# Spectral layer one sequence at a time, with output steps of sequence 0 between the mix items of sequence 1

## The chip, the cores and the metric

One core of one Trainium2 chip runs the whole program. The metric is device time in microseconds (us) of one execution. The kernel before was timed in three runs: 1540.98 us is the median, 1530.98 the lowest, 1542.16 the highest. A measurement of this kernel can tell about 1% (15.4 us) from no change.

## The reference: what is computed

Three layers run one after another; the change touches the first.

```python
# 1: spectral layer, x is (4 sequences, 3072 positions, 256)
X = np.fft.rfft(x, axis=1)
Yr = Xr @ w_r - Xi @ w_i + b_r
Yi = Xr @ w_i + Xi @ w_r + b_i
Yr, Yi = softshrink(Yr, 0.01), softshrink(Yi, 0.01)
y = np.fft.irfft(Yr + 1j * Yi, n=3072, axis=1)
# 2: top-1 mixture of 8 experts with a fixed capacity per expert (384 places)
# 3: dense mixture of 8 experts, weighted by a Sinkhorn-normalised gate
```

The places of layer 2 are given out in order of position, so with these inputs only the first two sequences (0 and 1) can hold a place; the kernel computes sequences 2 and 3 only in a branch that is taken if an expert is not full.

## The kernel before, in words

**The spectral layer** splits a 3072-point transform into 96 times 32. For each sequence there are four stages:

- `dft_in(b, i)`, 16 pieces: four matmuls on the input (tiles `xc`, four chunks of 8 rows per partition) with a 96-point matrix, split into a high and a low part (`z_hi`, `z_lo`) by ScalarE and VectorE.
- 24 *items* (b, u). `mix` multiplies by the weights: six matmuls of 512 columns (line 158). `fwd`: six matmuls of 256 columns with the matrix tile `mf` (line 179), then bias and soft shrink in `y` and `c` (lines 183 to 185; the last subtraction on VectorE for items that `solo` names, else on GpSimd). `shrink_split` splits `y` into `yh` and `yl`. `inv`: three matmuls of 256 columns with the matrix tile `mi` (line 200); ScalarE copies the result to `d` (line 202, two buffers), and SyncE's queue writes it to a DRAM tile `ds[b]` (line 203).
- A round trip through DRAM: `load_chunk` (line 118) reads `ds[b]` back in another order, as four chunks of 768 KB, into the same four `xc` tiles. A chunk holds rows of all 24 items, so the first chunk can be read only after the last item is written.
- `DftOut.step(k)`, 16 *output steps* per sequence, numbered through both sequences (k = 0 to 31, and two more that drain the pipeline). A step splits a piece of a chunk for step k + 2 (`dh`, `dl`), multiplies by `fi` (three matmuls of 512 columns, line 234), copies to `xo` (line 237) and writes `xs_d`, transposes the `xo` of step k - 1 (line 245), and multiplies the transposed piece of step k - 2 by the gate weights (`lps`, line 254). `out_step` adds the choice of experts for every fourth step (`choose`, `weigh`).

**The order** is written out by hand; each engine runs its instructions in program order. `mix_items` runs a software pipeline: iteration i issues `shrink_split` of item i - 4, `fwd` of i - 2, `mix` of i, `inv` of i - 5, three *fill* slots between them, and then a list `todo[i]`, which holds the loads of matrices, the loads of chunks and the output steps. `load_mats` runs on GpSimd's queue; with n buffers the load for a group waits until the group n places earlier has been used.

In the kernel before, the items run in five stretches: items 0 to 5 of sequence 0, the same of sequence 1, then items 6 to 13 of both in pairs that share one load of `mf` and `mi`, then 14 to 23 of sequence 0, and of sequence 1. So there are 40 groups of matrices for 48 items. Sequence 0 ends 10 items before sequence 1. Its first two chunks are read at iterations 42 and 43; output steps 0 to 5 stand at iterations 47 to 52, beside the last items, and steps 6 to 33 follow alone. Behind `mix_items` GpSimd clears `xg`, 128 x 6144 (line 534). The placing of tokens, the gather and the two expert layers follow; they are not touched.

## Time and profile before

| what | value |
|---|---|
| runs | 1530.98, 1540.98, 1542.16 us |
| profiled execution, span from first to last instruction | 1540.5 us |
| TensorE busy (matmul) | 1506.7 us, 98% |
| VectorE, ScalarE, GpSimd busy | 741.2, 484.9, 269.8 us |
| granted TensorE clock, mean | 0.958 of full speed |
| moved by DMA | 94.63 MB |

The profiled execution's time is given as its span alone; it lies 0.5 us below the median run, and nothing else is known to lie around it. Stretches are named by microseconds from the start of the span. The first transforms run to 22, the items and the transforms of sequence 1 from 28 to 163, the output steps to 273, the placing to 300, and the expert layers from 300 to the end. [...]

### The profile page before, as it was taken

To read this page: it belongs to the slowest core of one execution; us is meant where nothing else is said; L and a number is where in the kernel's file an instruction comes from. 1 tells how busy PE (TensorE), PEld (TensorE's weight loads), DVE (VectorE), ACT (ScalarE), POOL (GpSimd) and SP (SyncE) were. 2 spreads that over 40 slices of the span, in tenths; PEclk is the share of its full clock that TensorE was granted. 3 is DMA by queue.
4 is the path that set the end of the run, shared out by engine and by line. 5 is a ranking of instruction groups with operands and counts; after the bars stand their busy time and mean duration, and the time that the engine had idled before them with its cause. 6 is when DMAs were issued, how large, how long until landed. Compare 5 with 4: busy or idle time off the path is not lost.

```text
span 1540.5 us, 23165 instructions
## 1 busy us (share of the span) xinstructions
PE 1506.7 (98%) x9578; PEld 1376.4 (89%) x9578; DVE 741.2 (48%) x1451; ACT 484.9 (31%) x939; POOL 269.8 (18%) x330
## 2 busy tenths in 40 slices
PE   8999799799999999999999999999999999999998
PEld 7988688699999999999999999999999999999998
DVE  4768635665548444444444444444444444444443
ACT  3444554355542242222222222221222222132221
POOL 2354124642221010010101001010100101010122
PEclk8999855699999999999999999999999999999999
DMA  9447652353330220202000000000000000000000
GB/s 240 110 126 181 167 144 89 97 167 117 117 128 1 110 81 29 110 1 96 1 28 28 1 28 1 28 1 28 28 1 28 1 28 1 28 1 4 25 28 28
DMA packets 57159, 94.63 MB, mean 61 GB/s; under 512 B 5846, under 2 KB 39286, under 8 KB 55606
## 3 DMA queue, kind: packets, MB, share of 16 engines
q1 hardware_dynamic: 41622, 71.09, 14.7%
q0 software_dynamic: 14656, 21.71, 5.3%
q8 instruction: 76, 1.25, 0.3%
q10 hardware_dynamic: 768, 0.28, 0.1%
q14 instruction: 37, 0.30, 0.1%
HBM read 64.75 MB, written 28.31 MB: 60 GB/s over the span
## 4 chain that ended last, share of the span: by engine, by line
PE 78%; DMA 2%; issue 1%; POOLq 0%; DVE 0%; ACT 0%; ACTq 0%
PE ps_h L670 38%; PE ps_y L800 34%; PE ps_yT L694 4%; DMA out_dram<-acc,ido 1%; PE lg L679 1%; PE ps_t L658 0%; DMA xg<-xs_d,idx 0%; POOLq L959 0%; PE ps_s L771 0%; DVE hl L673 0%; ACT hh L672 0%; DVE xg L649 0%; ACT xgh L87 0%; POOLq L810 0%; PE ps_b L753 0%
## 5 line engine op out<-in xcount | busy, mean ns | idle before, releaser
L800 PE MATMUL ps_y<-w,hh 128*128 128x256 f32 x3072 | 557.3, 283 | 0.0
L672 ACT ACTIVATE hh<-ps_h 128x512 fp32r<-128x512 f32 (+2 forms) x456 | 262.8, 576 | 874.0 <-PE ps_h L670 873.6
L670 PE MATMUL ps_h<-x_hi,w 128*128 128x512 f32 (+1 forms) x1568 | 494.4, 387 | 0.0
L800 PEld LDWEIGHTS ps_y<-w,hh 128*128 128x128 f32 x3072 | 483.1, 189 | 7.7
L673 DVE SCALAR_TENSOR_TENSOR hl<-ps_h,hh 128x512 fp32r<-128x512 f32 (+2 forms) x456 | 301.8, 662 | 382.1 <-ACT hh L672 382.0
L800 PE MATMUL ps_y<-w,hl 128*128 128x256 f32 x1536 | 437.6, 285 | 0.0
L670 PEld LDWEIGHTS ps_h<-x_hi,w 128*128 128x128 f32 x1568 | 292.8, 188 | 58.4
L808 DVE SCALAR_TENSOR_TENSOR acc<-ps_y,pr,acc 128x256 f32<-128x256 f32 x360 | 174.2, 484 | 270.8 <-PE ps_y L800 259.6
L670 PE MATMUL ps_h<-x_lo,w 128*128 128x512 f32 (+1 forms) x784 | 303.5, 387 | 0.0
L800 PEld LDWEIGHTS ps_y<-w,hl 128*128 128x128 f32 x1536 | 290.3, 189 | 0.0
L88 POOL TENSOR_TENSOR w<-raw,w 128x512 fp32r<-128x512 f32 x84 | 109.4, 1304 | 953.9 <-ACT w L87 886.1
L670 PEld LDWEIGHTS ps_h<-x_lo,w 128*128 128x128 f32 x784 | 147.3, 188 | 25.5
L670 PE MATMUL ps_h<-xgh,w 128*128 128x384 f32 x256 | 78.0, 347 | 0.2 <-ACT xgh L87 0.2
L694 PE MATMUL ps_yT<-hh,w 128*128 128x384 f32 x256 | 75.8, 338 | 0.0
L87 ACT CAST w<-raw 128x512 fp32r<-128x512 f32 x124 | 75.5, 613 | 0.0
L670 PEld LDWEIGHTS ps_h<-xgh,w 128*128 128x128 f32 x256 | 48.0, 191 | 0.6 <-ACT xgh L87 0.6
L694 PEld LDWEIGHTS ps_yT<-hh,w 128*128 128x128 f32 x256 | 47.3, 188 | 0.0
L87 ACT CAST mh<-ps_m 128x512 fp32r<-128x512 f32 x48 | 28.2, 587 | 58.5 <-PE ps_m L158 58.5
L88 DVE TENSOR_TENSOR ml<-ps_m,mh 128x512 fp32r<-128x512 f32 x48 | 33.1, 690 | 27.6 <-ACT mh L87 27.6
L810 POOL DMA_INDIRECT out_dram<-acc,ido x24 | 23.4, 975 | 123.2 <-DVE acc L808 95.5
L670 PE MATMUL ps_h<-xgl,w 128*128 128x384 f32 x128 | 43.8, 342 | 0.0
L694 PE MATMUL ps_yT<-hl,w 128*128 128x384 f32 x128 | 43.2, 338 | 0.0
(169 smaller groups left out, 1313.4 us busy)
## 6 DMA issues: line engine op xcount, KB each, us to landing
raw<-in_moe_w_dram SPq DMA_DIRECT2D x60, 512.0 KB, 4.4
out_dram<-zt SPq DMA_DIRECT2D x24, 512.0 KB, 8.3
mf<-in_c_mats_dram POOLq DMA_DIRECT2D x40, 192.0 KB, 3.2
ds<-d SPq DMA_DIRECT2D x48, 128.0 KB, 2.7
xc<-ds SPq DMA_DIRECT2D x8, 768.0 KB, 5.9
xs_d<-xo SPq DMA_DIRECT2D x32, 192.0 KB, 2.1
xc<-in_x_dram SPq DMA_DIRECT2D x7, 768.0 KB, 12.7
mi<-in_c_mats_dram POOLq DMA_DIRECT2D x40, 128.0 KB, 2.9
```

The source lines that it names most:

```text
L87: nc.scalar.copy(hi_ap, src)
L88: (lo_engine or nc.vector).tensor_sub(lo_ap, src, hi_ap.bitcast(F32))
L670: nc.tensor.matmul(ps[:, 0:n], l, r[:, h, cols], start=k == 0, stop=k == 5)
L672: nc.scalar.activation(hh, ps[:, 0:n], AF.Relu)
L673: nc.vector.scalar_tensor_tensor(hl, ps[:, 0:n], 0.0, hh.bitcast(F32), op0=ALU.max, op1=ALU.subtract)
L679: nc.tensor.matmul(lg2[:, t, 0:m], src[:, h, c], wg2r[:, h, 0:m], start=i == 0, stop=i == 3)
L694: nc.tensor.matmul(yT[e][c], l, r, start=fk == 0 and i == 0, stop=fk == 2 * NF - 1 and i == 2)
L800: nc.tensor.matmul(ps, l, r, start=i == 0, stop=i == 3 * NF - 1)
L808: nc.vector.scalar_tensor_tensor(a, ps, pr[:, ti, e:e + 1], a, op0=ALU.mult, op1=ALU.add)
L810: nc.gpsimd.indirect_dma_start(out=out, out_offset=bass.IndirectOffsetOnAxis(ap=ido[:, ti % NCH, ti // NCH:ti // NCH + 1], axis=0), in_=a, ...
```

## The change

The items run one sequence at a time: 24 of sequence 0, then 24 of sequence 1, each with its own load of `mf` and `mi` (48 groups; `mf` has four buffers instead of five). The 16 `dft_in` pieces of sequence 1 are spread over 23 iterations instead of filling the first six. All four chunks of sequence 0 are read at iterations 29 and 30. Output steps 0 to 11 stand at iterations 32 to 51, between items of sequence 1. Two chunks of sequence 1 are read at iteration 52, the others in steps 12 and 15. Steps 12 to 33 follow `mix_items`. The last subtraction of the shrink goes to VectorE for four items only (26 before). `mh`, `ml` get three buffers and `dh`, `dl` two of their own (four shared before); `xo` has three instead of four.

```diff
-    mfp = s1.enter_context(tc.tile_pool(name="mfp", bufs=5))
+    mfp = s1.enter_context(tc.tile_pool(name="mfp", bufs=4))
...
-        mh = wk.tile([128, 2 * D], F32R, tag="mh", name="mh", bufs=4)
-        ml = wk.tile([128, 2 * D], F32R, tag="ml", name="ml", bufs=4)
+        mh = wk.tile([128, 2 * D], F32R, tag="mh", name="mh")
+        ml = wk.tile([128, 2 * D], F32R, tag="ml", name="ml")
...
-            dh = wk.tile([128, 2 * D], F32R, tag="mh", name="dh", bufs=4)
-            dl = wk.tile([128, 2 * D], F32R, tag="ml", name="dl", bufs=4)
+            dh = wk.tile([128, 2 * D], F32R, tag="dh", name="dh", bufs=2)
+            dl = wk.tile([128, 2 * D], F32R, tag="dl", name="dl", bufs=2)
...
-                o = w2p.tile([P1, 2, D], F32, tag="xo", name="xo", bufs=4)
+                o = w2p.tile([P1, 2, D], F32, tag="xo", name="xo", bufs=3)
...
-            todo.setdefault(max(last[g - 5] + 2, 0) if g >= 5 else 0, []).append(lambda g=g: load_mats(groups, g, True))
+            todo.setdefault(max(last[g - 4] + 2, 0) if g >= 4 else 0, []).append(lambda g=g: load_mats(groups, g, True))
...
-    UA, UB = 6, 14
-    items, groups = [], []
-    for b, u0, u1 in ((0, 0, UA), (1, 0, UA), (None, UA, UB), (0, UB, NU), (1, UB, NU)):
-        for u in range(u0, u1):
-            its = [(b, u)] if b is not None else [(0, u), (1, u)]
-            items += its
-            groups.append((u, its))
+    items = [(b, u) for b in range(NP) for u in range(NU)]
+    groups = [(u, [(b, u)]) for b, u in items]
...
-    i_d0 = items.index((0, NU - 1)) + 5
+    i_d0 = NU + 5
     todo = {}
     od = DftOut((0, 1))
-    todo.setdefault(i_d0, []).extend([lambda: load_chunk(ds[0], 0)])
-    todo.setdefault(i_d0 + 1, []).append(lambda: load_chunk(ds[0], 1))
-    early = [-1, 0, 1, 2, 3, 4]
-    for k, i in enumerate(early):
-        todo.setdefault(n_it + i, []).append(lambda k=k: out_step(k))
+    for g in range(4):
+        todo.setdefault(i_d0 + g // 2, []).append(lambda g=g: load_chunk(ds[0], g))
+    EARLY = 12
+    first = i_d0 + 3
+    for k in range(EARLY):
+        todo.setdefault(first + (k * (n_it + 5 - first)) // EARLY, []).append(lambda k=k: out_step(k))
+    for g in range(2):
+        todo.setdefault(n_it + 4, []).append(lambda g=g: load_chunk(ds[1], g))
...
-        if k in (1, 4):
-            load_chunk(ds[0], 2 + k // 4)
-        if k in (8, 9, 13, 17):
-            load_chunk(ds[1], (8, 9, 13, 17).index(k))
+        if k in (12, 15):
+            load_chunk(ds[1], 2 + (k - 12) // 3)
...
-    mix_items(items, groups, 2, 1, todo, solo=lambda i: UA <= i < 2 * UA or i >= n_it - 2 * (NU - UB),
-              fill=[lambda i=i: dft_in(1, i) for i in range(16)])
+    spread = []
+    for i in range(16):
+        spread += [lambda i=i: dft_in(1, i)] + [lambda: None] * (4 if i % 2 else 3)
+    mix_items(items, groups, 2, 1, todo, solo=lambda i: i >= n_it - 4, fill=spread)
```

**TensorE, output steps.** Before, from step 6 on, the steps of TensorE's queue stand one behind another (`ps_x` is the product of a step, `ps_t` its transposes, `lps` the gate logits):

```order
L234 MATMUL ps_x<-dh,fi 96x512
L234 MATMUL ps_x<-dl,fi 96x512
L234 MATMUL ps_x<-dh,fi 96x512
L245 MATMUL ps_t<-ident,xo 128x96 x4
L254 MATMUL lps<-wg1s,xT 96x8 x4
L234 MATMUL ps_x<-dh,fi 96x512
L234 MATMUL ps_x<-dl,fi 96x512
L234 MATMUL ps_x<-dh,fi 96x512
L245 MATMUL ps_t<-ident,xo 128x96 x4
L254 MATMUL lps<-wg1s,xT 96x8 x4
```

Now, at iterations 32 to 47, a step stands between the `inv` of one item and the `fwd` of another:

```order
L200 MATMUL ps_d<-yh,mi 128x256
L234 MATMUL ps_x<-dh,fi 96x512
L234 MATMUL ps_x<-dl,fi 96x512
L234 MATMUL ps_x<-dh,fi 96x512
L245 MATMUL ps_t<-ident,xo 128x96 x4
L254 MATMUL lps<-wg1s,xT 96x8 x4
L179 MATMUL ps_y<-mh,mf 128x256
L179 MATMUL ps_y<-ml,mf 128x256
L179 MATMUL ps_y<-mh,mf 128x256 x2
L179 MATMUL ps_y<-ml,mf 128x256
L179 MATMUL ps_y<-mh,mf 128x256
L158 MATMUL ps_m<-w_hi,z_hi 128x512
```

Nine steps (0 to 8) now stand ahead of the last `mix`, and three more (9 to 11) among the last `fwd` and `inv`; before, step 0 was the first behind the last `mix`.

**SyncE's queue, the read of sequence 0** (`ds_171` is `ds[0]`, `ds_172` is `ds[1]`, `xc0` to `xc3` are the chunks). Before, one write of an item stands between two chunks, and the other chunks come 8 and 15 rows later, between output steps:

```order
L203 DMA ds_171<-d_1937 128x256
L118 DMA xc0_111<-ds_171 96x2048
L203 DMA ds_172<-d_1976 128x256
L118 DMA xc1_112<-ds_171 96x2048
L203 DMA ds_172<-d_2015 128x256
L203 DMA ds_172<-d_2053 128x256
```

Now four chunks stand within seven rows:

```order
L203 DMA ds_172<-d_1473 128x256
L118 DMA xc0_111<-ds_171 96x2048
L118 DMA xc1_112<-ds_171 96x2048
L203 DMA ds_172<-d_1513 128x256
L118 DMA xc2_113<-ds_171 96x2048
L118 DMA xc3_114<-ds_171 96x2048
L203 DMA ds_172<-d_1553 128x256
L203 DMA ds_172<-d_1591 128x256
```

The first write behind a chunk now has two chunks ahead of it, and the next has four.

**GpSimd, the clearing of `xg`.** Before, it stands directly behind the last load of a matrix:

```order
L126 DMA mf<-in_c_mats_dram 128x384
L129 DMA mi<-in_c_mats_dram 128x256 x4
L534 MEMSET xg 128x6144
L291 CAST g_2396<-gw 96x8
L292 TENSOR_TENSOR r<-gw,g_2396 96x8
```

Now it stands behind the `weigh` of output step 11 (iteration 51), which needs `gw` from VectorE:

```order
L291 CAST g_2535<-gw 96x8
L292 TENSOR_TENSOR r<-gw,g_2535 96x8
L293 TENSOR_SCALAR g_2535<-r 96x8
L294 TENSOR_SCALAR r_2537<-g_2535 96x8
L295 TENSOR_TENSOR r_2537<-r_2537,r 96x8
L296 TENSOR_SCALAR g_2535<-r_2537 96x8
L299 TENSOR_TENSOR val<-oh,hc 96x64x2
L302 TENSOR_TENSOR val<-oh,g_2535 96x64x3
L532 MEMSET xg 128x6144
```

The clearing has moved from iteration 47 to behind the last output step of `mix_items`.

## Rows read from the trace of the kernel before

**Rows 1.** Busy time by stage (x instructions), PEclk granted clock, DMA share, GB/s.

```profile
27.95:158.00 130.05, 129.99 (x803) 116.52 (x803) 91.81 (x214) 58.45 (x144) 51.89 (x90) 0.97 0.61 150
158.00:163.20 5.20, 3.78 (x19) 2.59 (x18) 2.45 (x7) 2.24 (x6) 0.57 (x1) 1.00 0.94 228
163.20:171.10 7.90, 0.49 (x2) 0.18 (x2) 7.83 (x7) 1.50 (x4) 5.75 (x2) 0.78 0.17 51
174.50:184.60 10.10, 8.91 (x73) 7.74 (x72) 5.54 (x12) 7.48 (x19) 0.00 (x0) 1.00 0.67 197
184.60:272.90 88.30, 88.30 (x425) 75.20 (x425) 37.18 (x115) 44.07 (x90) 29.24 (x63) 0.50 0.42 122
```

**Rows 2.** TensorE in order of time: start, length, instruction; the last items.

```profile
153.42 0.28 PE L179 MATMUL ps_y<-mh,mf 128*128 128x256 f32 x1
...
154.13 0.40 PE L158 MATMUL ps_m<-w_hi,z_hi 128*128 128x512 f32 x1
...
155.53 0.28 PE L200 MATMUL ps_d<-yh,mi 128*128 128x256 f32 x1
...
155.89 0.28 PE L179 MATMUL ps_y<-mh,mf 128*128 128x256 f32 x1
...
157.77 0.40 PE L158 MATMUL ps_m<-w_hi,z_lo 128*128 128x512 f32 x1
```

**Rows 3.** TensorE in order of time, output steps beside the last items.

```profile
176.32 0.40 PE L234 MATMUL ps_x<-dh,fi 128*96 128x512 f32 x1
...
177.99 0.37 PE L200 MATMUL ps_d<-yh,mi 128*128 128x256 f32 x1
...
183.50 0.38 PE L200 MATMUL ps_d<-yh,mi 128*128 128x256 f32 x1 [1.19 <-ACT d L202]
```

**Rows 4.** TensorE in order of time, the last output steps.

```profile
264.70 0.84 PE L245 MATMUL ps_t<-ident,xo 96*128 96x96 f32 x4
...
266.53 0.72 PE L234 MATMUL ps_x<-dh,fi 128*96 128x512 f32 x1
...
269.73 0.88 PE L245 MATMUL ps_t<-ident,xo 96*128 96x96 f32 x4
```

**Rows 5.** SyncE's queue in order of time, around the first two chunk reads.

```profile
152.13 0.32 SPq L118 DMA_DIRECT2D xc<-ds  x1
152.51 0.42 SPq L203 DMA_DIRECT2D ds<-d  x1
152.97 0.43 SPq L118 DMA_DIRECT2D xc<-ds  x1
154.15 10.57 SPq L203 DMA_DIRECT2D ds<-d  x4
```

**Rows 6.** ScalarE in order of time: the copies to d behind those reads.

```profile
158.65 0.37 ACT L202 COPY d<-ps_d 128x256 f32<-128x256 f32 x1 [2.33 <-DMA ds<-d]
...
162.12 0.37 ACT L202 COPY d<-ps_d 128x256 f32<-128x256 f32 x1 [2.31 <-DMA ds<-d]
```

**Rows 7.** VectorE in order of time, at the clearing of xg.

```profile
163.63 5.74 DVE L184 TENSOR_SCALAR c<-y 128x256 f32<-128x256 f32 x1
```

**Rows 8.** GpSimd in order of time, the clearing of xg.

```profile
163.98 5.24 POOL L534 MEMSET xg<- 128x6144 f32 x1
```

**Rows 9.** The page's DMA issues: KB each, us to landing, writes of items.

```profile
ds<-d SPq DMA_DIRECT2D x48, 128.0 KB, 2.7
```

**Rows 10.** Tile xc, issue at 195.48: time to landing of one chunk read.

```profile
DMA to landing us min/median/max: 5.9/5.9/5.9
```

**Rows 11.** Groups by line, 184.60 to 272.90: count, busy us, mean ns, idle before.

```profile
L237 ACT COPY xo<-ps_x 96x512 f32<-96x512 f32 x27 | 15.7, 582 | 31.2 <-PE ps_x L234 31.2
L87 ACT CAST dh<-xc 128x512 fp32r<-128x512 f32 x25 | 15.5, 619 | 0.0
```

**Rows 12.** Groups by line, 60 to 158, GpSimd.

```profile
L129 POOL DMA_DIRECT2D mi<-in_c_mats_dram x32 | 17.2, 538 | 26.0 <-PE ps_d L200 26.0
L185 POOL TENSOR_TENSOR y<-y,c 128x256 f32<-128x256 f32 x18 | 13.2, 731 | 20.9 <-DVE c L184 20.9
```

More of the change, by code (lines that the diff above doesn't have):

```diff
@@ L604, in tile_spectral_mix__moe_topk__moe_sinkhorn @@
             for n in range(P2):
-                dp.onehot(n, w2p.tile([P1, cap], F16, tag="xo", name="at", bufs=4))
+                dp.onehot(n, w2p.tile([P1, cap], F16, tag="xo", name="at", bufs=3))
                 dp.invert(n)
```

## The prediction

> **What bounds the kernel now.** The page comes first: TensorE is busy 98% of the span, and the granted clock is 1.00 almost everywhere except between about 155 and 305. So the second view is busy time by stage. [...] While the items run, TensorE has no idle time: 129.99 of 130.05 us, at 0.97 [rows 1]. From 158.0 to 171.1 it works 3.78 + 0.49 of 13.1 us [rows 1]. [...]
>
> The order of time on TensorE then gives prices. An item takes 155.89 - 153.42 = 2.47 us, of which `fwd` 154.13 - 153.42 = 0.71 and `inv` 155.89 - 155.53 = 0.36 [rows 2]. An output step beside items takes 177.99 - 176.32 = 1.67 us at full clock [rows 1, 3]; alone at 0.50 it takes 269.73 - 266.53 = 3.20 us [rows 4]. The same work costs 1.53 us more there. ScalarE (44.07) and VectorE (37.18) have room in those 88.3 us [rows 1], so the clock sets the price of a step.
>
> The view of other engines says what made the hole at 158 to 171. Two writes of items queued with two chunk reads, and ScalarE waited 2.33 and 2.31 us for them before it could write `d` again [rows 5, 6]. Then GpSimd cleared `xg` for 5.24 us, and over the same time one VectorE operation of 128 x 256 took 5.74 us [rows 7, 8]; TensorE, behind it, idled and fell to half clock.
>
> **The change part by part.** I count from the end of the last `mix`. Its last matmul starts at 157.77, and the six of an item take 155.53 - 154.13 = 1.40 us, 0.23 each [rows 2], so that is 158.0; the steps end at 272.9. The kernel before needs 114.9 us for this stretch.
>
> *Work moved ahead.* Steps 0 to 8 now lie ahead of the last `mix`: 9 x 1.67 = 15.0 us of TensorE that were behind it. In an iteration with a step TensorE needs 2.47 + 1.67 = 4.14 us; GpSimd's part there is a subtraction of 0.73 and two issues of 0.54 [rows 12], and ScalarE adds copies of 0.58 and 0.62 [rows 11] and one of `xT`. None of them fills 4.14 us, so TensorE stays the bound, and the full price is paid.
>
> *Four chunk reads instead of two in the middle of the items.* Before, the write issued at 152.51 behind one chunk let ScalarE go on at 158.65, and the one at 154.15 behind two chunks at 162.12, that is 10.0 us after the first chunk's issue and 3.47 us after the other [rows 5, 6]. Now the first write stands behind two chunks: about 10.0 us after the first chunk's issue. Its buffer is wanted three items later, 7.4 us: a wait of 2.6. The next stands behind four: two more chunks, 2 x 3.47 = 6.9, so 16.9. It is wanted at 10.0 + 2.47 + 1.67 = 14.1: a wait of 2.8. TensorE stands behind ScalarE here. I take the whole 5.4 us as lost. The lower end is 1.4 us, what TensorE idled from 158.0 to 163.2 [rows 1]. The upper end is 12: if the loads of `mf` and `mi`, which go on now and had mostly ended at 152, share the transfers half and half, 2.6 and 2.8 about double.
>
> *The last iterations.* Behind the last `mix` come an `inv`, step 9, two `fwd`, five `inv` and steps 10 and 11: 6 x 0.36 + 2 x 0.71 + 3 x 1.67 = 8.6 us. The hole of 163.2 to 171.1 goes, since the clearing of `xg` waits for the `weigh` of step 11. What is late next is the round trip.
>
> *The round trip of sequence 1*, hidden before behind 16 steps of sequence 0. From the end of the last `inv`: the copy to `d` 0.6, its write 2.7 [rows 9], the issue 0.4 [rows 5], one chunk 5.9 [rows 10], then ScalarE's `dh` 0.62 and `xo` 0.58 [rows 11]: 10.8 us. It is `xo` of step 14 that waits, since step 14 asks for the split of step 16 first, and ScalarE runs in order. So TensorE has steps 12, 13, 14 and the three matmuls of step 15, 3 x 1.67 + 0.7 = 5.7 us, and then idles some 5 us. Four steps were moved there, but only these cover. A gap of 1.19 us before [rows 3] already ended in half clock: 1.00 up to 184.6, 0.50 behind it [rows 1]. So I take 0.50 from here on. From 10.8: the rest of step 15, 266.53 - 264.70 = 1.83 [rows 4]; steps 16 to 31, 16 x 3.20 = 51.2; the draining, 272.9 - 269.73 = 3.2 [rows 1, 4]. Sum 67.0 us.
>
> *The clearing of `xg`* now falls into that wait. The rows show that it held a VectorE operation with one tensor input [rows 7]; they do not show whether it holds the subtractions of `dl`. If not, it costs nothing. If it does, steps 14 and 15 come behind the wait at half clock, up to 2 x 3.20 - 1.83 = 4.6 us. I take nothing, since the wait for the chunk covers most of it. [...]
>
> *Edits that cost nothing.* The 22 subtractions moved from VectorE to GpSimd (0.73 us each) and the 8 more groups of matrices are covered by GpSimd's idle time, 51.89 of 130.05 us busy [rows 1, 12]; with the cover gone, `yh` would come late, and one item would lose up to 0.7 us. The `dft_in` pieces are the same TensorE work at other iterations. Fewer `mh`, `dh` and `xo` buffers: `dh` of step k + 2 now waits for step k's matmuls, for which `xo` waits anyway; `xo` of step 15 needs the write of step 12, which queues behind two chunks, and this ends about when the round trip does: 0 to 3 us.
>
> **Sum.** After: 15.0 + 5.4 + 8.6 + 67.0 = 96.0 us against 114.9, a gain of 18.9 us. The placing and the expert layers behind 272.9 are not touched. The profiled span of 1540.5 gives 1521.6; against the median run, 0.5 above it, **1522 us**.
>
> **The rivals.**
>
> *A: the full clock stays after the round trip.* [...] As a mechanism here: if steps in an unbroken row brought the clock back, 16 steps would save 1.53 each and the ends another 2.5, 27 us, for 1495. Against it speaks that 88.30 us of unbroken steps ran at 0.50 before and never rose [rows 1]. For it, that the gap may be shorter than 5 us, and that steps beside items kept 1.00 for 10 us [rows 1]. 10%.
>
> *B: the transfers eat the gain.* From iteration 29 to 39 the queues carry four chunks, ten items of 448 KB and five writes of 192 KB, about 8.7 MB, in some 33 us: 264 GB/s, above the 228 that the stretch with two chunks moved at a share of 0.94 [rows 1]. At 228 the same bytes take 38.2 us, so the middle loses 5.2 us or, with waits for `mf` on top, twice that, and the round trip 3 to 5 more. Result 1526 to 1540. 25%.
>
> *C: slower. The waits in the middle drop the clock and the items stay at half.* With one step every other iteration, repeated waits for `d` or `mf` would have to keep the clock from coming back. An item and a half step cost 2.47 + 0.84 = 3.3 us at full clock and about 6.5 at half. Over 6 such iterations the gain is gone, over 11 the kernel is 1% slower, over all 24 it would come to 1595. Against it: around 158 to 163 waits of over 2 us did not take the clock from 1.00 [rows 1, 6]. The price at 11 to 20 iterations is 1557 to 1585. 8%.
>
> *D: the change doesn't do what it says*: steps that stand among items wait there (on `xo`, `lps` or chunks) and TensorE gains nothing by the mixture. Each step would cost 3.20 as before, 12 x 1.53 = 18 us more, and the result is 1540. 4%.
>
> **How the numbers follow.** The forecast has 53%, with its own range 1511 to 1532: the bounds of the middle (-4, +7), the clearing and the `xo` buffers (up to +5 together), a chunk read of 4 instead of 5.9 us (-2), and a shorter or longer stretch of half clock. With A at 1495 and B up to 1540, the range that leaves out most of A and C is 1504 to 1541. About 1% (15.4 us) is what a measurement can tell, so faster means under 1525.6: three quarters of the forecast, all of A and a quarter of B, 0.56. Within 1%: the rest of the forecast and B, and D, 0.35. Slower: C and a rest, 0.09.
>
> **What would show it.** In the trace after: output steps of about 1.67 us between items from the middle of sequence 1 on; waits of ScalarE's `d` for `ds<-d` of 2 to 3 us, twice, behind the four chunks; no VectorE operation of 5 us ahead of the last `inv`; an idle stretch of about 5 us on TensorE behind step 14, with half clock from there until the placing ends; last step at about 254 instead of 272.9. A clock of 1.00 in steps 16 to 31 would make this wrong by A; long waits of `ps_y` on `mf`, or half clock among the items, by B or C.

## The result, and the profile after

The changed kernel took 1544.98 us (median of 19 runs, 1537.84 to 1550.44), the kernel before 1534.00 beside it (19 runs, 1525.18 to 1551.03): a ratio of 1.0075, 95% interval 1.0056 to 1.0093. It is slower by some 11 us, less than the 1% that a measurement of this kernel can tell from no change, where 1522 and a gain were predicted. Ratios and intervals leave out executions over 1.5% above the fastest of their kernel; of the kernel before, in the later series, these are executions with a mean granted clock of 0.959 or less. The profiled executions were 1540.5 us of span before and 1544.7 after.

One thing has to be known to read what follows: executions of the kernel before differ by up to 46 us (138 of them, in all series: 1510.65 to 1556.48), and the traces show two stretches in which they differ. The series ran on different chips (numbers in the table of the experiments; for the two first profiles the chip is not on record), and the median of the unaltered kernel before lies between 1522.1 and 1540.4 in the five later ones. So times and ratios of different series don't compare well, and most readings below go by the traces. Two marks cut a span into three parts: the end of the last logits matmul (L254, "steps' end") and the first expert matmul.

| us | before, shown | again_before | again_before2 | after | again_after |
|---|---|---|---|---|---|
| steps' end | 273.0 | 251.5 | 274.5 | 264.1 | 263.6 |
| first expert matmul | 298.0 | 276.5 | 299.7 | 288.6 | 289.4 |
| from there to the end | 1242.5 | 1254.9 | 1243.4 | 1256.1 | 1253.2 |
| span | 1540.5 | 1531.4 | 1543.1 | 1544.7 | 1542.6 |

Set against the execution that the prediction was made from, the first one of the changed kernel gains 8.9 us up to the steps' end and loses 13.6 behind the first expert matmul. Set against again_before, again_after loses 12.1 up to the steps' end, 12.9 up to the expert matmul, and gains 1.7 behind it: 11.2 in all. That the medians differ by as much is chance, since these are single executions.

Busy time of the changed kernel by stage (columns as in [rows 1]):

```profile
27.95:122.50 94.55, 94.21 (x593) 85.05 (x594) 60.70 (x139) 42.91 (x104) 51.95 (x87) 0.97 0.66 161
122.50:130.00 7.50, 0.53 (x4) 0.31 (x2) 0.74 (x2) 1.30 (x3) 1.77 (x3) 0.68 1.12 248
130.00:135.40 5.40, 5.17 (x15) 3.95 (x16) 3.04 (x6) 2.10 (x5) 0.56 (x1) 0.50 1.14 250
135.40:185.00 49.60, 49.16 (x330) 43.05 (x329) 33.01 (x75) 29.31 (x69) 25.85 (x49) 1.00 0.63 170
185.00:193.40 8.40, 6.45 (x53) 5.73 (x52) 6.62 (x19) 5.56 (x16) 0.31 (x1) 1.00 0.39 111
193.40:264.00 70.60, 70.60 (x340) 60.15 (x339) 29.64 (x94) 32.74 (x69) 28.71 (x56) 0.50 0.43 125
```

The hole of 163.2 to 171.1 [rows 1] is gone. A new one stands at 122.5 to 130.0. It comes from SyncE's queue and ScalarE's copies, which answer to [rows 5] and [rows 6]; in order of time, SyncE, ScalarE, TensorE:

```profile
116.84 0.79 SPq L118 DMA_DIRECT2D xc<-ds  x2
118.67 0.34 SPq L203 DMA_DIRECT2D ds<-d  x1
119.47 0.96 SPq L118 DMA_DIRECT2D xc<-ds  x2
121.13 0.34 SPq L203 DMA_DIRECT2D ds<-d  x1
...
129.29 0.37 ACT L202 COPY d<-ps_d 128x256 f32<-128x256 f32 x1 [5.99 <-DMA ds<-d]
...
130.23 0.74 PE L234 MATMUL ps_x<-dh,fi 128*96 128x512 f32 x1 [7.20 <-ACT dh L87]
```

Four reads of 768 KB stand around two writes. ScalarE waits 5.99 us for a `d` buffer, the `dh` of step 0 stands behind that wait on the same engine, and TensorE, at its first output step, idles 7.20 us. The clock falls to 0.50 in it and is back at 1.00 at 135.4, with items running.

The tail, TensorE (a step beside items, two waits in the last iterations, a late step), then GpSimd and VectorE at the clearing of `xg`, answering to [rows 3, 4, 7, 8]:

```profile
180.13 0.39 PE L234 MATMUL ps_x<-dh,fi 128*96 128x512 f32 x1
...
181.78 0.36 PE L179 MATMUL ps_y<-mh,mf 128*128 128x256 f32 x1
...
187.84 0.38 PE L179 MATMUL ps_y<-mh,mf 128*128 128x256 f32 x1 [0.57 <-DVE y L183]
...
192.64 0.38 PE L200 MATMUL ps_d<-yh,mi 128*128 128x256 f32 x1 [1.38 <-ACT d L202]
...
254.45 0.72 PE L234 MATMUL ps_x<-dh,fi 128*96 128x512 f32 x1
...
257.65 0.72 PE L234 MATMUL ps_x<-dh,fi 128*96 128x512 f32 x1
...
198.97 5.22 POOL L532 MEMSET xg<- 128x6144 f32 x1
...
199.03 0.69 DVE L88 TENSOR_TENSOR dl<-xc,dh 128x512 fp32r<-128x512 f32 x1 [2.65 <-ACT dh L87]
```

A step beside items took 1.65 us, a late one 3.20, as predicted. The clock fell behind the 1.38 us wait at 192.64 (1.00 up to 193.4, 0.50 from there), in the last iterations, not in the round trip.

Behind the steps, among the first expert products, a stretch with no counterpart in the first profile of before (ScalarE's `hh`, then the matmuls of TensorE around them, then busy time by stage):

```profile
310.11 0.49 ACT L670 ACTIVATE hh<-ps_h 128x384 fp32r<-128x384 f32 x1 [3.86 <-remote]
...
318.67 0.49 ACT L670 ACTIVATE hh<-ps_h 128x384 fp32r<-128x384 f32 x1 [7.56 <-remote]
...
307.18 0.34 PE L668 MATMUL ps_h<-xgh,w 128*128 128x384 f32 x1
...
310.65 0.69 PE L692 MATMUL ps_yT<-hh,w 128*128 128x384 f32 x1 [3.13 <-issue]
...
314.61 0.52 PE L668 MATMUL ps_h<-xgh,w 128*128 128x384 f32 x1
...
319.21 0.69 PE L692 MATMUL ps_yT<-hh,w 128*128 128x384 f32 x1 [4.08 <-ACT hh L670]
```

```profile
306.00:323.00 17.00, 9.74 (x30) 7.98 (x29) 5.57 (x11) 4.90 (x11) 9.53 (x10) 0.60 0.31 89
```

ScalarE waits 3.86 and 7.56 us for products whose last matmuls TensorE had started 2.9 and 4.1 us before (307.18 and 314.61); the view knows no releaser ("remote"). TensorE has 9.74 busy us in 17, at a mean clock of 0.60 (0.50 from 310 to 322). I call this the stop.

### The profile page after: what moved, and what is told of

Its sections match the earlier page's. It is cut to its first block, busy times and chain, and to the rows that moved or that the text cites. A ratio compares the mean times of both kernels' runs of the same rounds, so it can differ in the third digit from the quotient of the medians.

```text
span 1544.7 us, 23192 instructions
## 1 busy us (share of the span) xinstructions
PE 1502.2 (97%) x9578; PEld 1371.8 (89%) x9578; DVE 728.3 (47%) x1429; ACT 483.1 (31%) x939; POOL 290.5 (19%) x368
## 4 chain that ended last, share of the span: by engine, by line
PE 77%; DMA 2%; issue 1%; another core or an unknown queue 1%; ACT 0%; POOLq 0%; DVE 0%; ACTq 0%
PE ps_h L668 38%; PE ps_y L798 34%; PE ps_yT L692 4%; DMA out_dram<-acc,ido 2%; PE lg L677 1%; PE ps_t L656 0%; DMA xg<-xs_d,idx 0%; POOLq L957 0%; ACT hh L670 0%; PE ps_s L769 0%; DVE hl L671 0%; ACT w L87 0%; ACT xgh L87 0%; DVE xg L647 0%
## 5 line engine op out<-in xcount | busy, mean ns | idle before, releaser
L185 POOL TENSOR_TENSOR y<-y,c 128x256 f32<-128x256 f32 x44 | 32.2, 732 | 77.6 <-DVE c L184 69.4
```

Source lines behind the costliest of these rows:

```text
L185: sub.tensor_sub(y, y, c)
```

## The experiments

"Steps' end" and "rest" (first expert matmul to end) are of the profiled execution; times are the median and range of all runs; the interval is of the ratio to the kernel before in the same series. Runs on one chip are one series, but for after_best and best_three, which are a later one on chip 12.

| run | chip | steps' end | rest | time, us | interval |
|---|---|---|---|---|---|
| again_after | 11 | 263.6 | 1253.2 | 1544.5 | |
| again_before | 11 | 251.5 | 1254.9 | 1533.2 | |
| again_before2 | 12 | 274.5 | 1243.4 | 1545.0 | |
| chunks_apart | 11 | 261.3 | 1255.1 | 1543.6 (1537.8 to 1545.3) | 1.0013 to 1.0083 |
| tail_warm | 11 | 253.6 | 1255.2 | 1533.7 (1526.3 to 1550.9) | 0.9948 to 1.0029 |
| warm_gaps | 12 | 259.8 | 1243.8 | 1529.3 (1527.9 to 1532.3) | 1.0005 to 1.0068 |
| before_tail_warm | 12 | 241.8 | 1244.2 | 1516.9 (1513.0 to 1521.1) | 0.9909 to 0.9975 |
| gathers_late | 12 | 262.9 | 1243.7 | 1532.9 (1529.4 to 1535.4) | 0.9998 to 1.0063 |
| chunks_gathers | 4 | 260.4 | 1243.9 | 1531.8 (1529.5 to 1534.8) | 0.9985 to 1.0071 |
| before_gathers | 4 | 260.7 | 1243.8 | 1524.7 (1515.9 to 1543.5) | 0.9909 to 0.9992 |
| loads_sp | 2 | 265.7 | 1243.8 | 1533.7 (1531.9 to 1538.4) | 1.0051 to 1.0109 |
| before_fill | 2 | 253.3 | 1243.0 | 1519.0 (1516.7 to 1523.5) | 0.9948 to 1.0019 |
| before_warm_gathers | 4 | 246.9 | 1243.4 | 1517.0 (1510.4 to 1517.8, 4 runs) | 0.9815 to 0.9979 |
| after_warm_all | 4 | 250.6 | 1244.2 | 1521.8 (1519.1 to 1544.9) | 0.9951 to 1.0008 |
| after_best | 12 | 245.9 | 1244.8 | 1517.8 (1515.7 to 1521.7) | 0.9937 to 1.0004 |
| best_five | 2 | 243.4 | 1243.6 | 1510.4 (1509.2 to 1514.0) | 0.9885 to 0.9947 |
| best_two | 2 | 236.9 | 1243.6 | 1515.3 (1507.1 to 1518.0) | 0.9923 to 0.9987 |
| best_three | 12 | 247.4 | 1243.0 | 1517.4 (1513.9 to 1523.6) | 0.9956 to 1.0013 |

### Is the profile the kernel?

Both kernels again, unaltered.

> The changed kernel again, unaltered. Its first profile shows ScalarE stopping twice before an L670 hh among the first expert matmuls (3.86 and 7.56 us, TensorE idle with it, clock 0.50 from 310 to 322), although hh waits for matmuls that had ended; from the first L668 matmul to the end of the span that execution took 1256.2 us, the kernel before 1242.5. Theory A (the stop belongs to this kernel): both stops are there again, the stretch takes 1254 to 1258 us, the span is 1542 to 1548. Rival B (an accident of one execution): no L670 wait over 2 us, the stretch takes 1241 to 1245 us, the span 1531 to 1536.

> The kernel before again, unaltered. Its first profile (1540.98 us) is slower than the median of its runs (1534.0). Theory A: what differs between executions lies in the expert layers, since nothing ahead of them waits for an outside event: steps end at 272 to 274 us again, and a shorter span comes from the stretch after the first expert matmul (1242.5 us in the first profile) or from the wait ahead of it (ScalarE 11.07 us for a weight transfer up to 297.49). Rival B: the steps' end itself moves by over 3 us from one execution to the next.

> The kernel before a third time. Its two profiles had the steps end at 272.9 and 251.4 us: in the first the clock fell to 0.50 at 184.8 us, one microsecond after a wait of 1.19 us for a d copy, in the second there was no such wait and it fell at 216 us, after one of 0.75 us. Theory A (this wait comes and goes between executions, and the clock with it): the steps' end is near 251 without the wait and near 273 with it. Rival B (the clock falls at times unrelated to waits): it falls with no TensorE gap of 0.5 us or more in the 3 us before.

The changed kernel repeated itself, as theory A had it: stop, steps' end, span (the rest, 1253.2, is just under A's 1254). The kernel before did not. In again_before theory A fell and rival B held: the steps' end moved by 21.5 us, and the stop, absent from the first profile, was there. Its TensorE at the last `inv` and at a later wait, its ScalarE at the stop, and its tail by stage:

```profile
184.85 0.39 PE L200 MATMUL ps_d<-yh,mi 128*128 128x256 f32 x1
...
185.19 0.28 PE L200 MATMUL ps_d<-yh,mi 128*128 128x256 f32 x1
...
214.37 0.17 PE L319 MATMUL bs<-tot,hc 96*96 96x8 f16 x1 [0.75 <-DVE tot L311]
...
306.19 0.49 ACT L672 ACTIVATE hh<-ps_h 128x384 fp32r<-128x384 f32 x1 [8.35 <-remote]
```

```profile
180.00:196.00 16.00, 16.00 (x141) 13.98 (x140) 8.75 (x20) 13.83 (x32) 2.93 (x8) 1.00 0.80 226
196.00:212.00 16.00, 15.65 (x136) 13.14 (x135) 10.46 (x30) 12.82 (x31) 6.72 (x18) 1.00 0.94 273
212.00:216.00 4.00, 3.25 (x30) 2.69 (x28) 3.79 (x8) 3.26 (x8) 3.18 (x7) 1.00 0.66 205
216.00:220.00 4.00, 4.00 (x21) 3.35 (x20) 3.90 (x9) 1.90 (x4) 2.20 (x4) 0.51 0.38 99
220.00:251.00 31.00, 31.00 (x153) 26.63 (x152) 14.96 (x55) 14.39 (x29) 14.59 (x28) 0.50 0.30 92
```

From the end of the last `inv` (185.5) to 216.0, for 30.5 us, output steps alone held a clock of 1.00, where [rows 1] has 0.50; it fell behind the wait of 0.75 us, to 0.51. In this execution TensorE did not wait for `d` at 184.85. In again_before2 it did, and the clock fell there, to 0.50 from 186 on, as theory A said:

```profile
184.78 0.38 PE L200 MATMUL ps_d<-yh,mi 128*128 128x256 f32 x1 [1.24 <-ACT d L202]
```

```profile
186.00:216.00 30.00, 30.00 (x144) 25.35 (x142) 10.24 (x27) 16.20 (x35) 5.20 (x16) 0.50 0.59 165
```

The early fall is the rarer case: the two profiles that have it show mean granted clocks of 0.958 and 0.957, and of 100 other executions of the kernel before, in the four later series on chips 12, 4 and 2, 25 lie at 0.960 or less.

### The clock in the tail

Matmuls that compute nothing are added. tail_warm (changed kernel) and before_tail_warm (kernel before) have them in the last iterations and in the steps:

```diff
+    def warm(n):
+        ps = p1.tile([128, D], F32, tag="y", name="ps_z")
+        for _ in range(n):
+            nc.tensor.matmul(ps, zer_h, iota[:, 0:D], start=True, stop=True)
...
+            if n == 48 and i >= n + 2:
+                warm(8)
             if i >= 5:
                 inv(*items[i - 5])
...
     def out_step(k):
+        if k >= EARLY and k != 21:   # before_tail_warm: k >= 6
+            warm(5)
         od.step(k)
```

> The changed kernel with added matmuls that compute nothing (128x96 weights of zero, 256 columns, their result read by nobody): eight in each of the last three iterations, five ahead of every output step from the 13th on but one. Theory A (the steps after the items cost 3.20 us because TensorE's clock is granted at 0.50 there, and it falls because the steps alone leave TensorE idle or thinly used): the clock stays at 1.00 from 193 us on, a step takes about 2.2 us (1.67 and five matmuls of 0.11), the steps end at 238 to 248 us in place of 264.0. Rival B (the half clock comes from something the added matmuls don't change): the clock still falls at 193 to 200 us, a step takes 3.2 + 5 x 0.21 = 4.3 us, and the steps end at 282 to 290 us, the time 1560 to 1575 us. Under A the time is 1520 to 1530 us if the expert layers are as in the changed kernel's first profile.

> The kernel before with the same added matmuls as in the changed kernel's tail_warm: eight in each of the last three iterations, five ahead of every output step from the seventh on but one. Theory A (the clock in the tail, not the order of items and steps, decides which of the two kernels is faster): the clock is 1.00 for most of the tail, the steps end at 240 to 250 us, and the time is within 0.5 per cent of tail_warm's 1533.7, so that what the change does to the order is worth less than 8 us. Rival B (the order itself is worth the 15 us that nine steps cost): the steps end 12 to 18 us later than tail_warm's 253, at 265 to 271, and the time is 1544 to 1552.

warm_gaps keeps the first edit, and in place of the second has `warm(32)` ahead of step 16 and `warm(10)` ahead of `dp0.place2()`. before_fill is before_gathers (below) with the first edit alone.

> The changed kernel with matmuls that compute nothing put only where TensorE idled or is about to: eight in each of the last three iterations (the 1.38 us wait at 192.64, after which the clock fell), 32 (about 3.5 us) ahead of the 17th step, the first that reads sequence 1, and ten ahead of the placing matmul of step 21. None in the other steps. Theory A (steps alone keep the full clock as long as TensorE does not idle for more than half a microsecond or so, but do not win it back): clock 1.00 past 193 us up to the 17th step at least, steps of 1.67 us there; if the fills cover all gaps, to the end, and the steps end at 226 to 238 us in place of 264. If one gap stays open the clock falls there and the rest of the steps take 3.20 us: end at 240 to 255. Rival B (steps alone lose the clock whatever the gaps): clock 0.50 at 193 to 197 us as before, end of the steps at 262 to 268, and the time no better than the changed kernel's 1545.

> before_gathers with eight added matmuls in each of the last three iterations and none in the steps: TensorE has work during the 1.2 us wait for a d copy at 184 us. before_gathers had three groups of times (1516 to 1522, 1528 to 1531, one at 1543). Theory A (the wait at 184 us is what makes the slowest group, the clock falling there and the steps ending near 273): no time over 1535, the other two groups stay. Rival B (the clock falls there for another reason): times at 1540 to 1545 as often as in the kernel before, about one in four.

In tail_warm the clock passed 193 at 1.00, fell in the round trip, to 0.52 from 206, and was back at 1.00 from 223.6, with the added matmuls beside the steps (ScalarE's wait, TensorE's, then the stages):

```profile
204.66 0.62 ACT L87 CAST dh<-xc 128x512 fp32r<-128x512 f32 x1 [4.97 <-DMA xc<-ds]
...
205.81 0.30 PE L245 MATMUL ps_t<-ident,xo 96*128 96x96 f32 x1 [3.25 <-ACT xo L237]
```

```profile
190.00:200.00 10.00, 10.00 (x90) 8.76 (x89) 4.49 (x13) 6.40 (x16) 5.02 (x9) 1.00 0.33 92
...
206.00:223.60 17.60, 17.43 (x88) 14.27 (x88) 5.85 (x22) 7.48 (x17) 3.55 (x10) 0.52 0.57 170
223.60:250.00 26.40, 26.10 (x233) 22.22 (x233) 19.36 (x60) 17.01 (x37) 17.64 (x30) 1.00 0.43 130
```

That is the round trip of the prediction: `dh` of step 16 waits 4.97 us for its chunk, `xo` of step 14 stands behind it. Its end, 253.6, missed theory A's 238 to 248 for it. warm_gaps, without help in the steps, kept 1.00 past 193 too, so the fall at 193.4 goes with the wait; my fill for the round trip stood one step late, the wait there came to 4.70 us, and the end, at 259.8, lies between theory A and rival B. There the clock fell at 207, behind the wait of 4.70, and came back beside the 32 added matmuls (0.66 from 208.0 to 216.8, 1.00 from there to 222), and held for steps alone up to a wait of 0.71 us at 230.29. Of warm_gaps' lower time, 9 to 12 us are the absent stop (rest 1243.8 against 1253.2 and 1256.1). before_fill took the group of times at 1540 and above away: all ten runs within 1516.7 to 1523.5, where 8 of 31 of the kernel before beside it lie at 1536 or above. The group at 1528 to 1531, which theory A had staying, is missing too. And before_tail_warm was not within 0.5% of tail_warm but 17 us faster, in another series; between their profiles, 22 us apart, 11 are the stop, which tail_warm's has. Five matmuls a step are no surety: two of tail_warm's ten runs took 1551 us at a mean clock of 0.965 and less, where the others have 0.977 and more, and no trace shows why.

Steps alone did not bring the clock back in any trace (0.50 over all of 88.30 us in [rows 1], over 70.60 in the changed kernel). Nor did each gap drop it. In the ten profiles without added matmuls, from 175 us on, it passed every TensorE gap of up to 0.57 us and fell at the first of 0.74 us or more (before_gathers' at 204.74 is the smallest); best_two, with two added matmuls a step, passed one of 1.83 us at 224.69 at 1.00.

### The middle

chunks_apart spaces the reads: `todo.setdefault(i_d0 + 5 * g, [])` in place of `i_d0 + g // 2`.

> The changed kernel with one edit: the four chunk reads of sequence 0 are issued five iterations apart (one at i_d0, then i_d0+5, +10, +15) in place of two and two in adjoining iterations. Theory A (the reads issued in a bunch hold the d writes behind them, ScalarE waits 6.0 us for a d buffer, and with it TensorE 7.2 us, after which it works at the half clock for some 5 us): ScalarE's wait at d falls below 2 us, TensorE's 7.2 us at the first ps_x goes, the clock stays at 1.00, and the last mix ends at 172 to 178 us in place of 184.0; steps end at 252 to 258 in place of 264.0. Rival B (TensorE waits there for the first chunk itself, which lands some 8 us after its issue whatever follows it): the wait for dh stays above 4 us and the last mix moves by less than 3 us. For the time, 1533 to 1539 us if the expert layers are as in the changed kernel's first profile; 1542 to 1548 if these hand the gain back.

The wait for `d` fell to 1.55 us and the clock stayed at 1.00 to 190, but the last `mix` came only 3.0 us earlier, at 181.2: theory A's signs without its size (172 to 178). The second read, issued at 135.09, now stood 2.1 us ahead of the `dh` that wanted it, and made its own wait (ScalarE, TensorE):

```profile
141.05 0.62 ACT L87 CAST dh<-xc 128x512 fp32r<-128x512 f32 x1 [3.87 <-DMA xc<-ds]
...
143.68 0.39 PE L179 MATMUL ps_y<-mh,mf 128*128 128x256 f32 x1 [2.86 <-DVE y L183]
```

With reads at 0, 2, 8 and 14 iterations (after_best) the last `mix` ended at 175.4, 8.8 us earlier than in the changed kernel: theory A's place and size, one spacing later.

### The stop

gathers_late moves the gathers of experts 2 to 7 into the expert loop; chunks_gathers and before_gathers do the same in chunks_apart and in the kernel before. loads_sp leaves the run of 24 gathers in chunks_apart and moves the weight loads that stand between them to SyncE (`load_w(e + 1)`).

```diff
-    for e in range(E):
+    for e in range(2):
         gather(e, xs_d[:, :], NP * SEQ, idx)
...
                 fk = NF * h + f
+                if fk == 0 and e + 2 < E:
+                    gather(e + 2, xs_d[:, :], NP * SEQ, idx)
```

> The changed kernel with the 18 row gathers of experts 2 to 7 issued inside the expert loop, three at the first product of the expert two ahead, in place of all 24 in one run of 35 us on GpSimd's queue. Theory A (TensorE's stop among the first expert products, 10 to 13 us with the cold clock after it, comes from the gathers that run beside it: it ended within 3 us of the last gather in five executions): ScalarE no longer waits over 2.5 us for a product between the first L668 matmul and 45 us after it, the stretch from the first of these matmuls to the end of the span takes 1241 to 1245 us in place of 1253 to 1256, and the time is 1530 to 1536 us. Rival B (the weight transfers, or the products' own order, cause it): a stop of 5 us or more remains, the stretch takes 1252 to 1257 us, the time 1542 to 1547.

> chunks_apart and gathers_late together: the changed kernel with the chunk reads of sequence 0 five iterations apart and the gathers of experts 2 to 7 in the expert loop. chunks_apart alone had all its times between 1537.8 and 1545.3 us, and its profile the stop among the first expert products. Theory A (without a run of gathers beside them the first expert products don't stop): all times 12 to 13 us lower, 1526 to 1533, and 1241 to 1245 us from the first expert matmul to the end. Rival B (the stop's absence in gathers_late was a matter of the moment at which the expert layers began, some microseconds later or earlier than elsewhere): times of 1538 to 1545 again, or spread over both.

> The kernel before with the gathers of experts 2 to 7 in the expert loop and nothing else changed. Theory A (the kernel before varies for two reasons: a wait of 1.2 us near 184 us that drops the clock for the rest of the steps or does not, worth 21.5 us, and a stop among the first expert products, worth 12.5, which this edit takes away): times in two groups, at 1519 to 1523 (steps end near 251) and at 1540 to 1545 (near 273), none between 1526 and 1537. Rival B (the two go together, or there is a third cause): times all through the range of the kernel before, 1511 to 1556.

> chunks_apart, whose executions all had the stop among the first expert products, with the weight loads of the second and third half expert issued by SP ahead of all gathers in place of by GpSimd between them. The 24 gathers stay in one run. Theory A (the run of gathers is enough for the stop): times of 1537 to 1546 as in chunks_apart. Rival B (it takes weight loads on the same queue between the gathers): no stop, 1526 to 1535.

The same stage as above, in gathers_late:

```profile
306.00:323.00 17.00, 17.00 (x105) 16.97 (x104) 11.13 (x21) 8.90 (x19) 0.00 (x0) 1.00 0.41 125
```

All ten runs of gathers_late lie below all 19 of the changed kernel, all ten of chunks_gathers below all ten of chunks_apart, by 12 us in the median, and none of the profiles with either edit has the stop. But these comparisons cross series, and the unaltered kernel before differs as much between them: its median is 1540.4 on chip 11, beside chunks_apart, and 1529.2 on chip 4, beside chunks_gathers. In before_gathers the times fell into three groups, not two: 1516 to 1522, 1528 to 1531, one at 1543. Its profile, 1529.0 of span, is of the middle one, with the clock falling at 205.5.

What starts the stop is open. It stood in 5 of 20 profiles (rest 1253.2 to 1256.1), in the others the rest took 1242.5 to 1244.8: it costs some 11 us. Four of the five are all the profiles made on chip 11, again_before among them; the fifth is the first of the changed kernel. None of the 14 made on chips 12, 4 and 2 has it, and three of these (again_before2, warm_gaps, before_tail_warm) have neither edit. So the stop goes with the series, perhaps with the chip, and since neither edit was run on chip 11, it is not shown that either takes it away. The times agree: at a mean granted clock of 0.964 the kernel before took 1538.6 to 1541.0 us on chip 11, 1533.0 and 1533.6 on chips 4 and 12. The moment at which the expert layers begin does not decide it: they began at 278.1 us with a stop (tail_warm) and at 278.6 without (before_fill).

### What the order is worth, and a faster kernel

before_warm_gathers joins before_tail_warm and the late gathers; after_warm_all joins tail_warm, chunks_apart and the late gathers; after_best is that with reads at 0, 2, 8, 14 and `warm(32)` ahead of step 15.

> before_tail_warm with the gathers of experts 2 to 7 in the expert loop. before_tail_warm had no stop in its profile and 1516.9 us. Theory A: nothing left for this edit to take away, 1512 to 1520 us. Rival B (some of its executions did stop, or the gathers in the loop cost something of their own): over 4 us to either side.

> The changed kernel with everything that was found: chunk reads five iterations apart, the added matmuls of tail_warm, gathers of experts 2 to 7 in the expert loop. Together with before_warm_gathers it compares the two orders with the clock held and without the stop. Theory A (the order of the change is itself a little worse: the steps of sequence 0 that it spends among the items were what covered the reading of sequence 1, and ScalarE now waits 5.0 us for its first chunk): steps end at 249 to 253 us, 5 to 10 later than before_warm_gathers, and the time is 1519 to 1524 us. Rival B (the order is worth its predicted gain once clock and stop are out of the way): 1500 to 1512 us.

> after_warm_all with its two remaining TensorE gaps treated: chunk reads at iterations 0, 2, 8 and 14 behind i_d0 (the second came 1.5 iterations ahead of its first use and ScalarE waited 3.9 us for it), and 32 added matmuls ahead of output step 15 in place of five, where ScalarE's wait for the first chunk of sequence 1 left TensorE idle for 2.1 to 4.7 us and the clock fell. Theory A (with every gap filled the order of the change is as good as that of the kernel before, not better): steps end at 241 to 246 us, as in best_five (243.4), and 1508 to 1514 us. Rival B (its order is worth its predicted 19 us once the clock holds): below 1500. Rival C (the round trip that its own steps no longer cover stays a loss): steps end at 247 to 252, 1515 to 1521.

The first two came out at theory A's times, 1517.0 (four runs) and 1521.8; but after_warm_all's steps end 3.7 us later than before_warm_gathers', not 5 to 10. after_best's times fit its rival C, its steps' end lies at A's upper end, and it did not hold the clock: from a wait of 1.48 us on, for an `xo` of the round trip (to 204.95), the clock was at 0.50 up to 218.2.

```profile
204.00:220.00 16.00, 15.05 (x82) 12.58 (x83) 4.50 (x15) 7.21 (x16) 4.62 (x10) 0.57 0.37 107
```

best_five is before_warm_gathers with the memset moved; best_two and best_three have two and three added matmuls a step.

```diff
-    nc.gpsimd.memset(xg, 0.0)
...
         out_step(k)
+        if k == 12:
+            nc.gpsimd.memset(xg, 0.0)
```

> before_warm_gathers with the memset of xg issued behind output step 12 in place of ahead of step 6. In two of the three profiles of the kernel before and in before_warm_gathers VectorE's c (L184) took some 6 us beside that memset and TensorE idled 5.6 to 6.4 us for the dl behind it. Theory A (the memset at its old place is what holds VectorE, and at the new one no clamp of an item runs beside it): no TensorE gap over 2 us near 170, steps end 4 to 6 us earlier than before_warm_gathers, 1508 to 1513 us. Rival B (the memset holds something else where it stands now): a gap of 3 us or more beside it, 1515 to 1519.

> best_five with two added matmuls a step in place of five. Theory A (steps keep the full clock without help as long as no gap opens, so three matmuls of 0.11 us less in some 27 steps are a gain of up to 9 us): 1502 to 1508 us, clock 1.00 in the steps. Rival B (two a step are too few to keep the clock over the small gaps of 0.5 to 0.9 us, or to win it back): it falls to 0.50 somewhere between 175 and 216 and stays there; steps after it take 3.4 us or more; 1518 to 1545, spread.

> best_five with three added matmuls a step in place of five. Theory A (three are enough to hold the clock over the gaps that best_two lost it at): 1505 to 1509 us, in one group. Rival B (the gaps of 0.7 to 1.8 us that faster steps open drop the clock in some executions, as in best_two): spread over 1507 to 1518.

best_five's tail by stage:

```profile
163.50:171.00 7.50, 5.12 (x22) 3.67 (x21) 5.47 (x13) 4.87 (x11) 0.58 (x1) 0.81 0.31 88
171.00:176.00 5.00, 5.00 (x42) 4.54 (x41) 3.13 (x8) 3.70 (x10) 0.00 (x0) 0.94 0.76 190
176.00:243.00 67.00, 66.16 (x609) 57.95 (x607) 41.21 (x117) 44.68 (x98) 34.73 (x63) 1.00 0.60 174
```

The hole beside the memset is gone and the clock stays at 1.00 to the steps' end. At 1510.4 us, 0.9916 (0.9885 to 0.9947) of the kernel before, it is faster than that kernel, and its ten runs lie within 4.8 us; best_two was faster in its profile (236.9) but spread over 11 us. Three a step, in another series, did worse than five: its clock fell at 229, behind a gap of 1.73 us. So with added matmuls and the stop away, the best try with the order of the change ends its steps 2.4 us later than the best with that of before (245.9 against 243.4) and takes 1517.8 against 1510.4, in different series. (best_five's profiled execution, 1514.0, is the slowest of its ten.) What the order of the change is worth with the clock held through its round trip, no run shows.

## Why the prediction was wrong

The sum gave a span of 1521.6 us, the profile shows 1544.7. Of the 23.1 us between them, 10.1 arose up to the steps' end (264.1 instead of 254.0) and 13.6 behind the first expert matmul; the stretch between took 0.6 less.

**The step that failed is the first one: that the 88.30 us at half clock [rows 1] are how the kernel before runs.** The gain of 18.9 us was mostly this: steps moved from 3.20 to 1.67 us, and the hole beside the memset. In again_before the same steps ran at 1.00 up to 216 and ended 21.5 us earlier, 12.1 ahead of again_after's. Whether the wait of 1.2 us [rows 3] drops the clock early comes out anew in each execution, in about one of four as in the profile; the sum took it as given. The prediction even used that row, for the kernel after. The changed kernel, whose clock fell at 193 to 195 in both of its profiles, ends its steps between the two ends that the kernel before has.

**"The placing and the expert layers behind 272.9 are not touched"** failed too, a term put at nothing that came to 13.6 us: 1256.1 and 1253.2 us there, against 1242.5 without the stop. The instructions are the same; that a stretch's code is unchanged did not make its time unchanged. It explains the loss against the profile shown and over half of the distance to 1522, not the loss against the median, since the kernel before stops in some executions as well; in how many of those timed beside the changed kernel is not known.

**The start of the count** was misread: the last `mix` of before ends at 162.55, not at 158.0, as this row of its TensorE shows; the item in between was left out, 2.5 us.

```profile
162.15 0.40 PE L158 MATMUL ps_m<-w_hi,z_lo 128*128 128x512 f32 x1
```

**The chunk reads in the middle**: right place and cause, wrong size. Two waits of 2.6 and 2.8 were one of 5.99: the buffer behind two chunks came free 12.5 us after the first chunk's issue (129.29 - 116.84), not 10.0, and was wanted after 6.5, not 7.4. The cold clock behind it was not priced. Of 122.5 to 135.4, 12.9 us, the work fills 0.53 + 5.17 / 2 = 3.1 at full clock: 9.8 lost instead of 5.4, within the bounds of 1.4 to 12. These 4.4 and the item's 2.5 more than cover the 5.7 by which the last `mix`, at 184.1, came later than 178.4.

**Steps beside items** cost 1.65 (predicted 1.67), so rival D falls; the clock came back among items, so rival C falls (its price for all 24 iterations is 1599 by its own 3.2 us each, not 1595). That the clock is at 0.50 from the round trip on was right in effect but not in cause: it fell earlier, in the last iterations, which the sum had at full clock. Steps 12 to 15 then took 3.20 each, long enough to hide the round trip. From the last `mix` to the steps' end this came to 80.0 us against 75.6. Where the clock was held up to it, the idle time appeared, 3.25 us in tail_warm.

**The clearing of `xg`** was right: the hole went, and the `dl` beside it took 0.69 us. So the 4.6 us did not occur, and best_five shows the same move in the kernel before, whose hole went as well (TensorE busy 5.12 of 7.50 us from 163.5 on, against 0.49 of 7.90 [rows 1]).

**Rival A** did not come about: 70.60 us of steps stayed at 0.50. That steps in an unbroken row bring the clock back was the author's supposition, and no trace here shows it: the clock came back to 1.00 among items (at 135.4) and beside added matmuls (at 223.6 in tail_warm), not in steps alone. Of rival B, the middle cost is there; it was not the larger part.

## What to carry to other kernels

Take a second profile of the kernel before, and look at the spread of its times, before pricing a stage: a gain that rests on a stage's granted clock is only as sure as the wait that set that clock. Set a run against the unaltered kernel in the same series before calling an edit the cause: the stop came and went with the series. Where work does not win a lost clock back, as the steps here (0.50 for 70.60 us), fill the small waits ahead of it first; on this kernel a few empty matmuls (before_tail_warm, 0.9909 to 0.9975) were worth more than a new order of the work (1.0056 to 1.0093). Steps moved into another stage also leave a place empty: what they covered there, here the round trip of sequence 1, becomes a wait (3.25 us of TensorE in tail_warm).

## What the runs showed of the hardware

Output steps alone held a clock of 1.00 for 30.5 us (again_before) and did not regain it in 88.3 at 0.50 [rows 1]. The first expert products stopped, ScalarE waiting up to 8.35 us for matmuls that TensorE had issued, in some executions of one program and not in others (again_before on chip 11, with 1254.9 us from the first expert matmul to the end; again_before2 on chip 12, with 1243.4); with the cold clock behind it that cost some 11 us.
